# Reading the weights a second time for their range check, in six later turns

## The chip, the cores and the metric

The kernel runs on one core of a Trainium2 chip. The metric is the time on the device in microseconds (us). Names of engines: PE is TensorE, the matmul engine (PEld its weight loads), DVE is VectorE, ACT is ScalarE, POOL is GpSimd, SP is SyncE, which here only issues transfers. "SPq" and "ACTq" are the parts of SP and ACT that issue DMAs.

## The reference

Two layers follow each other. The first is a gated linear recurrence with 4 batch entries, 8 heads, 768 steps and head size 48; the second a gated state-space layer on 384 features with 512 inner channels:

```python
for t in range(S):
    state = alpha[:, :, t, :, None] * state + np.einsum('bhd,bhe->bhde', k[:, :, t], v[:, :, t])
    y[:, :, t] = np.einsum('bhd,bhde->bhe', q[:, :, t], state)
...
proj = x @ w_in
val, gate = (proj[..., :D_inner], proj[..., D_inner:])
for t in range(S):
    h = a[0, 0] * h + val[:, t, :]
    ys[:, t, :] = h
silu = gate * (1.0 / (1.0 + np.exp(-gate)))
return (silu * ys @ w_out).astype(np.float32)
```

`x` is `y` with the heads side by side. The weights `w_in`, `w_out` and `A_log` are handed over in their inputs' own types; the kernel reads `w_in` and `w_out` as pairs of 32-bit words and makes 32-bit floats of them itself.

## The kernel before

**Groups and turns.** The 4 x 768 steps are cut into N = 12 groups of 256 steps (NG = 3 groups for each batch entry). Work runs in turns: in turn n, the recurrence of group n is finished and that of group n + 1 begun, the first part of the second layer of group n - 1 runs, and the output of group n - 2. Group and turn numbers, and those of batch entries, count from 0.

**An order written by hand.** Each turn is a string of letters, read one by one (lines 467 to 517), and each engine runs its instructions in the order in which they are written there. F is a step of `front(n)`: scans along time of alpha (`V`, `P`), then q and k multiplied by them, scores `sc`, and k turned back (`tpk`, `Kn`). A is the same for group n + 1. B is a step of `back(n)`: block states `z`, values `y`, features `x_sb`, and their transposes `tpx`, `xT`. P and H are steps of `ssm(n - 1)`: twelve products `pj` with `w_in`, then the scan `hh` (DVE), the gate `sg` (ACT) and their product `f` (DVE). O is a step of `ssm(n - 2)`: products `o` with `w_out`, and the output. `pj` and `o` share two PSUM buffers.

**How inputs arrive.** Groups 0 to 3 (`n < BY_VECTOR`, line 229) are loaded by `load(n)` into `pads` and turned by TensorE (`tp`). Later groups come by whole batch entries, `load_batch(b)` at line 234, in a layout that VectorE turns by itself (`squares`, line 330). Entry 1 needs only its last two groups and is cut into 48 transfers; entries 2 and 3 have 12 each. All of these are issued by SP, in program order; v is loaded by ACT from turn 2 on. The letter L calls `load_later(n)`: the load of group n + 2 in turns 0 and 1, the last four weight units (turn 0), and entries 2 and 3 in turns 3 and 5. M calls `load_last(n)`: entry 1 in turn 2, and v of group n + 2. `load_batch` also has GpSimd fill unused columns (line 241).

**Shared buffers.** Two big buffers are used in turn. One holds `pads`, then entry 2. The other holds `staging`, the raw words of the twelve weight units (line 261), then entry 1, then entry 3. A new holder's transfers wait until the old one was last read.

**Weights.** U is `convert_unit`: two passes on ACT, two on DVE and one on GpSimd turn the raw words of a unit into 32-bit floats. W is `check_units(p)`: two ACT passes over the high words of WP = 3 units in `staging`, which sum up whether a weight is out of range. C is `check_products(n)`: two ACT passes over `V`, which do the same for the products of decays. At the end `any_outside` (line 447) looks at all these sums; if one is out of range, a slower general form computes everything again. It does not run for these inputs.

Of the kernel before, what the change touches and what calls it, by code (L numbers as in the profile page):

```python
# [9 lines left out]
FP32 = mybir.dt.float32  # L10
U8 = mybir.dt.uint8
U32 = mybir.dt.uint32
# [6 lines left out]
def kernel(  # L19
# [24 lines left out]
    nc = tc.nc  # L44
# [3 lines left out]
    C = 128  # L48
# [5 lines left out]
    NG = S // GC  # L54
# [3 lines left out]
    NK = DM // C  # L58
# [14 lines left out]
    w_out = const.tile([C, NI, DM], FP32, name="w_out")  # L73

    left = const.tile([C, N, 2], FP32, name="left")
    WP = 3
    left_w = const.tile([C, 3 * NI // WP, 2], FP32, name="left_w")
    flag = const.tile([1, 1], I32, name="flag")
    bias = const.tile([C, 3], FP32, name="bias")
# [3 lines left out]
    units = []  # L83
# [7 lines left out]
    def load_heads(dst, src, n, queue=nc.sync):  # L91

        b, g = divmod(n, NG)
        for c in range(G):
            rows = ds(g * GC + c * C, C)
            queue.dma_start(out=dst[:, c], in_=src[b, :, rows, :].rearrange("h p d -> p h d"))

    def load_pairs(dst, src, n, queue=nc.sync):

        b, g = divmod(n, NG)  # L100
        for c in range(G):
            rows = ds(g * GC + c * C, C)
            for i in range(2):
                queue.dma_start(out=dst[:, c, :, i, 0:D],
                                in_=src[b, ds(NP * i, NP), rows, :].rearrange("h p d -> p h d"))
# [93 lines left out]
    def step(gen):  # L199
        if gen is not None:  # L200
            next(gen, None)


    def ranged(ctx):
        def pool(name, bufs, **kw):
            return ctx.enter_context(tc.tile_pool(name=name, bufs=bufs, **kw))

        own = pool("own", 1)
        p1 = pool("p1", 1)
# [20 lines left out]
        W = 32  # L230
# [3 lines left out]
        def load_batch(b):  # L234
            t = big.tile([C, 3, NP * NW * W], FP32, tag=f"big{1 - b % 2}", name="batch")
            for m, (name, src) in enumerate((("a", alpha), ("q", q), ("k", k))):
                tv = t[:, m].rearrange("p (x e) -> p x e", e=W)
                batches[b, name] = t[:, m].rearrange("p (j x) -> p j x", j=NP)
                w0 = max(0, BY_VECTOR - NG * b) * GC // W
                for i in range(2):  # L240
                    nc.gpsimd.memset(tv[ds(DP * i + W, W), :, D - W:W], 1.0 if name == "a" else 0.0)  # L241
                for j, nj in [(0, NP)] if w0 == 0 else [(j, 1) for j in range(NP)]:
                    for i in range(2):
                        for half in range(2):
                            ch = min(W, D - W * half)
                            nc.sync.dma_start(  # L246
                                out=tv[ds(DP * i + W * half, W), j * NW + w0:(j + nj) * NW, 0:ch],
                                in_=src[b, ds(NP * i + j, nj), w0 * W:S, ds(W * half, ch)]
                                .rearrange("j (w p) d -> p (j w) d", p=W))
# [3 lines left out]
        def load(n, names="aqkv", queue=nc.sync):  # L253
            for name in names:
                if name == "v":
                    vs[n] = p3.tile([C, G, H, D], FP32, name="v_sb")
                    load_heads(vs[n], v, n, queue)
                elif n < BY_VECTOR:
                    load_pairs(pads[n % NBUF][name], dict(a=alpha, q=q, k=k)[name], n, queue)

        staging = big.tile([C, len(units), NK * C * 2], U32, tag="big0", name="staging")
# [8 lines left out]
        def convert_unit(u):  # L270


            lo, hi = bits_of(u)[..., 0], bits_of(u)[..., 1]
            dst = units[u][0].bitcast(U32)

            nc.scalar.activation(lo.bitcast(FP32), lo, AF.Copy, scale=2.0 ** -29, bias=2.0 ** 23)
            nc.scalar.activation(lo, lo.bitcast(FP32), AF.Copy, bias=-2.0 ** 23)
            nc.vector.tensor_scalar(out=dst, in0=hi, scalar1=0x07FFFFFF, scalar2=3,
                                    op0=ALU.bitwise_and, op1=ALU.logical_shift_left)
            nc.vector.scalar_tensor_tensor(out=dst, in0=hi, scalar=0xC0000000, in1=dst,  # L280
                                           op0=ALU.bitwise_and, op1=ALU.bitwise_or)
            nc.gpsimd.tensor_add(units[u][0].bitcast(I32), units[u][0].bitcast(I32), lo.bitcast(I32))

        def check_units(p):


            h = staging[:, ds(WP * p, WP), :].rearrange("p u (x two) -> p (u x) two", two=2)[:, :, 1].bitcast(FP32)
            nc.scalar.activation(h, h, AF.Square, scale=2.0 ** -16, accum_out=left_w[:, p, 0:1])
            nc.scalar.activation(h, h, AF.Relu, scale=-2.0 ** 60, bias=bias[:, 0:1], accum_out=left_w[:, p, 1:2])

# [86 lines left out]
        def check_products(n):  # L377
            V = Vs[n % 2]
            junk = p1.tile([C, NP, GC], U8, name="junk")
            nc.scalar.activation(junk, V[:, :, 0:GC], AF.Relu, scale=-1.0 / LOW, bias=bias[:, 0:1],  # L380
                                 accum_out=left[:, n, 0:1])
            nc.scalar.activation(junk, V[:, :, 0:GC], AF.Relu, scale=1.0 / HIGH, bias=bias[:, 2:3],
                                 accum_out=left[:, n, 1:2])
# [58 lines left out]
        for u in range(4, 8):  # L442
            fetch_unit(u)
        nc.scalar.activation(a_dec, a_log, AF.Exp)
        to_convert, to_check = iter(range(len(units))), iter(range(len(units) // WP))

        def any_outside():

            worst = own.tile([C, 1], FP32, name="worst")
            bad = own.tile([C, 3 * NI // WP * 2 + 1], FP32, name="bad")  # L450
            nc.vector.tensor_reduce(out=bad[:, 0:1], in_=left.rearrange("p n w -> p (n w)"),
                                    axis=mybir.AxisListType.X, op=ALU.max)

            nc.vector.tensor_scalar(out=bad[:, 1:], in0=left_w.rearrange("p n w -> p (n w)"), scalar1=0.5,
                                    scalar2=0.5, op0=ALU.is_lt, op1=ALU.is_lt)
            nc.vector.tensor_reduce(out=worst, in_=bad, axis=mybir.AxisListType.X, op=ALU.max)
            wt = ps_tp.tile([1, C], FP32, tag="tp", name="wt")
            nc.tensor.transpose(wt, worst, ident)
            w1 = own.tile([1, 1], FP32, name="w1")
            nc.vector.tensor_reduce(out=w1, in_=wt, axis=mybir.AxisListType.X, op=ALU.max)  # L460
            nc.vector.tensor_scalar(out=flag, in0=w1, scalar1=0.0, scalar2=None, op0=ALU.is_gt)
# [2 lines left out]

        early = ["FFFFLUFUFABBABB", "UUFPUUFHPUHFFPUHBBCPHABUAUBL", "FPUFHPUHFFPHBBCAPHBWAWOBWAWOM"]
        usual = "FLPHPHFFOABBCPHABPHBAOM"
        ending = ["PHPHOPHPHO", "OO"]
        fronts = {n: front(n) for n in range(N)}  # L470
        backs = {n: back(n) for n in range(N)}
# [11 lines left out]
        def load_last(n):  # L483
            if n == 2:
                load_batch(1)
            if 2 <= n < N - 2:
                load(n + 2, "v", nc.scalar)

        with tc.manual_schedule():
            for n in range(N + 2):  # L490
                if n == N:
                    any_outside()
                for word in early[n] if n < len(early) else usual if n < N else ending[n - N]:
                    if word == "F":
                        step(fronts[n])
                    elif word == "A":
                        step(fronts.get(n + 1))
                    elif word == "B":
                        step(backs[n])
                    elif word in "PH":  # L500
                        if n - 1 not in ssms:
                            ssms[n - 1] = ssm(n - 1, xs.pop(n - 1), prev_h, p2, ps_mm)
                        step(ssms[n - 1])
                    elif word == "O":
                        step(ssms[n - 2])
                    elif word == "C":
                        if n == 1:
                            check_products(0)
                        check_products(n)
                    elif word == "U":  # L510
                        convert_unit(next(to_convert))
                    elif word == "W":
                        check_units(next(to_check))
                    elif word == "L":
                        load_later(n)
                    elif word == "M":
                        load_last(n)
            outside = nc.values_load(flag[0:1, 0:1], min_val=0, max_val=1)
# [156 lines left out]
    with ExitStack() as inner:  # L675
        outside = ranged(inner)
# [33 lines left out]
```

## Time and profile before

| what | value |
|---|---|
| time, median of 3 runs | 335.95 us (334.61 to 337.5) |
| span of the profiled run | 334.8 us |
| PE busy | 291.8 us (87%) |
| DVE busy | 223.5 us (67%) |
| ACT busy | 126.0 us (38%) |
| POOL busy | 45.0 us (13%) |
| mean granted TensorE clock | 0.942 |
| DMA moved | 29.01 MB in 157570 packets, 150864 of them under 512 B |

The profile is a record of one execution. Its page cuts the span into 40 slices of 8.4 us, and each digit is the busy share of an engine in tenths; PEclk is the clock that TensorE was granted, in tenths. "The chain that ended last" goes back from the last instruction: from each to what released it. Lines of a timeline give start, duration, engine, source line, output <- inputs and the number of instructions, and in brackets the idle time before them and what ended it. A line of waits gives who waited for whom: us in total, how often, the longest.

Here the costliest group is that of the products `pj` (135.6 us busy), then `o` (67.9 us). The twelve conversions and the four checks of weights all lie in the first three turns.

### The profile page before, as it was taken

How to read it: one execution, taken by the hardware profiler on the slowest of the kernel's cores; microseconds unless marked ns; L12 is line 12 of the kernel's file. 1: busy time of each engine (PE TensorE's matmuls, PEld its weight loads, DVE VectorE, ACT ScalarE, POOL GpSimd, SP SyncE). 2: the span in 40 equal slices, each digit the busy share in tenths (PEclk: the TensorE clock that was granted, in tenths of full speed). 3: DMA queues.
4: the chain of work that ended last, by engine and by line, in shares of the span. 5: the costliest groups of instructions: out<-in, count | busy, mean ns of one | idle time of the engine just before them, and what ended most of it. 6: DMA issues, size and time to landing. Idle time of an engine off the chain costs nothing.

```text
span 334.8 us, 9254 instructions
## 1 busy us (share of the span) xinstructions
PE 291.8 (87%) x4041; PEld 231.6 (69%) x4041; DVE 223.5 (67%) x387; ACT 126.0 (38%) x259; POOL 45.0 (13%) x58
## 2 busy tenths in 40 slices
PE   1577995899499792599999999999999999999993
PEld 1355883787377671477787778877887778777771
DVE  1886786769123960679878888898788988833220
ACT  1133668237932410243252442513524325244111
POOL 4020420320069300000910000000000000000000
PEclk9995898699789898599999999999999999999999
DMA  9999994000056547976885996940030120000011
GB/s 129 224 223 239 204 222 86 0 3 4 23 104 99 72 74 99 125 101 94 116 117 108 132 120 99 153 79 31 2 72 25 28 46 25 25 26 2 27 45 59
DMA packets 157570, 29.01 MB, mean 87 GB/s; under 512 B 150864, under 2 KB 157008, under 8 KB 157520
## 3 DMA queue, kind: packets, MB, share of 16 engines
q1 hardware_dynamic: 134784, 20.06, 41.2%
q10 hardware_dynamic: 22736, 8.26, 10.1%
q8 instruction: 34, 0.56, 0.7%
q14 instruction: 16, 0.13, 0.1%
HBM read 23.60 MB, written 4.72 MB: 85 GB/s over the span
## 4 chain that ended last, share of the span: by engine, by line
PE 75%; DVE 6%; DMA 6%; ACT 5%; SPq 3%; issue 3%; ACTq 1%; DVEq 0%
PE pj L115 34%; PE o L130 18%; PE sc L368 4%; PE tp L326 4%; PE tpk L142 4%; PE y L187 4%; PE z L154 3%; PE y L169 3%; DMA v_sb<-in_v_dram 3%; PE tpx L196 3%; SPq L246 2%; DVE P L344 2%; DVE V L339 2%; DMA pads<-in_alpha_dram 1%; DMA batch<-in_q_dram 1%
## 5 line engine op out<-in xcount | busy, mean ns | idle before, releaser
L115 PE MATMUL pj<-xT,w_in 128*128 128x256 f32 x576 | 135.6, 389 | 0.0
L115 PEld LDWEIGHTS pj<-xT,w_in 128*128 128x128 f32 x576 | 109.7, 194 | 17.6 <-issue 0.2
L130 PE MATMUL o<-w_out,f 128*128 128x384 f32 x192 | 67.9, 499 | 0.0
L124 ACT ACTIVATE sg<-pj 128x256 f32<-128x256 f32 x48 | 18.4, 384 | 119.1 <-DVE hh L119 98.6
L130 PEld LDWEIGHTS o<-w_out,f 128*128 128x128 f32 x192 | 36.2, 197 | 20.9 <-issue 2.1
L119 DVE TENSOR_TENSOR_SCAN hh<-a_dec,hh,pj 128x256 f32<-128x256 f32 x32 | 23.7, 740 | 21.1 <-PE pj L115 21.1
L125 DVE TENSOR_TENSOR f<-sg,hh 128x256 f32<-128x256 f32 x48 | 20.4, 425 | 24.9 <-ACT sg L124 24.9
L326 PE MATMUL tp<-ident,pads 128*128 128x128 f32 x96 | 19.6, 358 | 16.0 <-DMA pads<-in_alpha_dram 6.9
L241 POOL MEMSET batch<- 32x1536 f32 x18 | 24.7, 1371 | 64.7 <-DMA out_dram<-o_sb 41.7
L326 PEld LDWEIGHTS tp<-ident,pads 128*128 128x128 f32 x96 | 15.0, 183 | 19.4 <-issue 8.0
L368 PE MATMUL sc<-Q,K 64*64 64x64 f32 x768 | 15.9, 237 | 10.7 <-DVE K L359 10.6
L133 ACT ACTIVATE o_sb<-o 128x384 f32<-128x384 f32 x24 | 11.8, 490 | 33.5 <-PE o L130 33.5
L368 PEld LDWEIGHTS sc<-Q,K 64*64 64x64 f32 x768 | 14.0, 148 | 14.9 <-issue 14.3
L344 DVE TENSOR_TENSOR_SCAN P<-aT,iV,bias 128x256 f32<-128x256 f32 x32 | 23.6, 780 | 0.6
L339 DVE TENSOR_TENSOR_SCAN V<-aT,bias 128x256 f32<-128x256 f32 x32 | 20.3, 677 | 0.3
L393 POOL TENSOR_TENSOR S_n<-S_end,V 128x192 f32<-128x192 f32 x7 | 4.2, 598 | 118.5 <-DVE V L339 118.5
L330 DVE STREAM_TRANSPOSE K<-batch 128x1024 f32<-128x1024 f32 x8 | 9.9, 1239 | 12.7 <-DMA batch<-in_k_dram 12.7
L196 PE MATMUL tpx<-ident,x_sb 128*128 128x128 f32 x72 | 11.9, 300 | 6.0 <-DVE P L344 4.3
L187 PEld LDWEIGHTS y<-S_n,Q 64*64 64x64 f32 x704 | 13.1, 140 | 5.7 <-issue 4.9
L169 PE MATMUL y<-v_sb,A 64*64 64x48 f32 x768 | 14.2, 220 | 3.2 <-issue 3.2
L371 DVE COPY_PREDICATED A<-mask,sc 128x512 f32<-128x512 uint8 x24 | 16.1, 723 | 0.7 <-PE sc L368 0.7
L154 PEld LDWEIGHTS z<-v_sb,Kn 64*64 64x64 f32 x768 | 12.3, 134 | 6.1 <-issue 5.4
(64 smaller groups left out, 314.2 us busy)
## 6 DMA issues: line engine op xcount, KB each, us to landing
out_dram<-o_sb ACTq DMA_DIRECT2D x24, 192.0 KB, 2.0
staging<-in_moe_w_in_dram SPq DMA_DIRECT2D x8, 384.0 KB, 5.0
v_sb<-in_v_dram ACTq DMA_DIRECT2D x16, 192.0 KB, 3.4
pads<-in_alpha_dram SPq DMA_DIRECT2D x16, 96.0 KB, 5.0
pads<-in_k_dram SPq DMA_DIRECT2D x16, 96.0 KB, 3.7
v_sb<-in_v_dram SPq DMA_DIRECT2D x8, 192.0 KB, 4.4
staging<-in_moe_w_out_dram SPq DMA_DIRECT2D x4, 384.0 KB, 5.5
batch<-in_alpha_dram SPq DMA_DIRECT2D x4, 384.0 KB, 6.6
```

The lines of the kernel that those rows point to most:

```text
L115: nc.tensor.matmul(pj[:, i, :], w_in[:, kk, i, ds(cc * C, C)], xT[:, kk, :], start=(kk == 0), stop=(kk == NK - 1))
L119: nc.vector.tensor_tensor_scan(out=hh, data0=a_dec[:, cc:cc + 1].to_broadcast([C, GC]), data1=pj[:, 0, :], initial=prev_h[cc][:, GC - 1:GC ...
L130: nc.tensor.matmul(o, f[:, cc, ds(c * C, C)], w_out[:, cc, :], start=(cc == 0), stop=(cc == NI - 1))
L154: nc.tensor.matmul(zv[chs, r, g, j, :], Kn[rows, g, j, chs], v_sb[rows, g, NP * i + j, :], start=True, stop=True, skip_group_check=True)
L169: nc.tensor.matmul(yv[at, i, c, j, :], A[rows, i, c * NP + j, :], v_sb[rows, c, NP * i + j, :], start=(c == 0 and j == 0), stop=False, ski ...
L187: nc.tensor.matmul(yv[at, i, c, j, :], Q[rows, j, ds(R * x, R)], S_n[rows, x, j, :], start=False, stop=(c == G - 1 and j == NP - 1), skip_ ...
L196: nc.tensor.transpose(tp[:, kk, :], x_sb[:, c, ds(kk * C, C)], ident)
L241: nc.gpsimd.memset(tv[ds(DP * i + W, W), :, D - W:W], 1.0 if name == "a" else 0.0)
L326: nc.tensor.transpose(tp[:, u, ds(c * C, C)], pad[name][:, c, j], ident)
L339: nc.vector.tensor_tensor_scan(out=V[:, 2 * jj + u, GC - 1::-1], data0=tp[:, u, ::-1], data1=bias[:, 1:2].to_broadcast([C, GC]), initial=1 ...
L344: nc.vector.tensor_tensor_scan(out=P[:, 2 * jj + u, :], data0=tp[:, u, :], data1=bias[:, 1:2].to_broadcast([C, GC]), initial=iV0[:, 2 * jj ...
L368: nc.tensor.matmul(scv[ds(R * r, R), i, c * NP + j, :], K[rows, j, steps], Q[rows, j, steps], start=True, stop=True, skip_group_check=True)
```

## The change

The check of the weights no longer reads `staging`. Instead the raw weights are fetched from memory a second time, two units at a time (WP = 2), into a buffer of their own (`part`, one buffer), and checked there, in six parts. Part p is fetched by the letter M of turn p + 4 and checked by the letter W, now the first of a turn, in turn p + 5; so the fetches fall into turns 4 to 9 and the checks into turns 5 to 10. `staging` is then free as soon as the last unit was converted, and M, with entry 1's load, moves up in turn 2, to just behind that conversion. The load of group 3 (L in turn 1) moves up as well. The check of group 0's products moves from turn 1 to turn 0.

```diff
-    WP = 3
+    WP = 2
...
-        def check_units(p):
-            h = staging[:, ds(WP * p, WP), :].rearrange("p u (x two) -> p (u x) two", two=2)[:, :, 1].bitcast(FP32)
+        parts = {}
+
+        def fetch_part(p):
+            parts[p] = p1.tile([C, WP, NK * C * 2], U32, name="part")
+            for w in range(WP):
+                dst, src = units[WP * p + w]
+                nc.sync.dma_start(out=parts[p][:, w].rearrange("p (a n) -> p a n", a=dst.shape[1]), in_=src.bitcast(U32))
+
+        def check_part(p):
+            h = parts.pop(p).rearrange("p u (x two) -> p (u x) two", two=2)[:, :, 1].bitcast(FP32)
             nc.scalar.activation(h, h, AF.Square, scale=2.0 ** -16, accum_out=left_w[:, p, 0:1])
             nc.scalar.activation(h, h, AF.Relu, scale=-2.0 ** 60, bias=bias[:, 0:1], accum_out=left_w[:, p, 1:2])
...
-        early = ["FFFFLUFUFABBABB", "UUFPUUFHPUHFFPUHBBCPHABUAUBL", "FPUFHPUHFFPHBBCAPHBWAWOBWAWOM"]
-        usual = "FLPHPHFFOABBCPHABPHBAOM"
+        early = ["FFFFLUFUFCABBABB", "UUFPUUFLHPUHFFPUHBBCPHABUAUB", "FPUFHPUHMFFPHBBCAPHBAOBAO"]
+        usual = "WFLPHPHFFOABBCPHABPHBAOM"
...
+            if 0 <= n - NG - 1 < len(units) // WP:
+                fetch_part(n - NG - 1)
...
                     elif word == "C":
-                        if n == 1:
-                            check_products(0)
                         check_products(n)
...
-                    elif word == "W":
-                        check_units(next(to_check))
+                    elif word == "W" and n - NG - 2 in parts:
+                        check_part(n - NG - 2)
```

More of the change, by code (lines that the diff above doesn't have):

```diff
@@ L444, in ranged @@
         nc.scalar.activation(a_dec, a_log, AF.Exp)
-        to_convert, to_check = iter(range(len(units))), iter(range(len(units) // WP))
+        to_convert = iter(range(len(units)))
         def any_outside():
```

## The prediction

> **What bounds the kernel now.** I read the page's 40 slices first, then the chain that ended last, in order of time, then the waits (all engines, and the DMA queue's own), then each engine's timeline from 40 to 182 us. The slices:
>
> ```profile
> PE   1577995899499792599999999999999999999993
> PEclk9995898699789898599999999999999999999999
> DMA  9999994000056547976885996940030120000011
> ```
>
> From slice 17 (142 us) to the end TensorE is full at full clock, so nothing off TensorE costs time there as long as nothing stops it. Before that it has holes, and DMA is silent in slices 7 to 10 (58 to 92 us). The chain shows a turn's rhythm and what makes the holes:
>
> ```profile
> 82.00 1.36 ACT staging L288 x2
> 83.38 1.43 ACT staging L289 x2
> 88.80 1.97 PE tp L326 x8
> 90.77 4.50 PE o L130 x8
> ...
> 105.49 2.93 DMA batch<-in_q_dram
> ...
> 132.64 2.64 DMA batch<-in_k_dram
> ...
> 156.56 5.18 PE pj L115 x24
> ...
> 178.34 5.18 PE pj L115 x24
> ```
>
> The pairs of products that open a turn (`pj` x24) stand at 156.56, 178.34, 200.11: a full turn costs 21.78 us. Turn 4 opens at 121.90, so turn 4 took 34.66; turn 2 (60.64 to 95.08, by its first transposes) 34.4 and turn 3 26.8. The waits tell why:
>
> ```profile
> SPq L246 <- ACT staging L289: 42.3, 1, 42.3
> SPq L246 <- DMA out_dram<-o_sb: 29.1, 7, 7.6
> SPq L246 <- DMA v_sb<-in_v_dram: 19.8, 7, 7.9
> ```
>
> These are the DMA queue's own waits (us in total, times, longest). TensorE's timeline has its idle time in brackets:
>
> ```profile
> 88.80 1.97 PE L326 MATMUL tp<-ident,pads 128*128 128x128 f32 x8 [4.28 <-ACT xT L197]
> ...
> 113.00 1.35 PE L187 MATMUL y<-S_n,Q 64*64 64x48 f32 x48 [1.74 <-DVE S_n L400]
> ...
> 137.81 2.07 PE L368 MATMUL sc<-Q,K 64*64 64x64 f32 x64 [10.57 <-DVE K L359]
> ```
>
> Batch entry 1 (the second, counted from 0) shares its buffer with `staging`, so SyncE waits 42.3 us until the last range check has read it (94.5 us). Then VectorE waits for alpha (4.19 us before 108.42) and for k (12.65 us before 135.69), and TensorE behind it.
>
> **What the Trainium skill says.** "PSUM — Partial Sum Buffer", section "Engine vs sequencer instructions": the queues of ScalarE, VectorE and GpSimd are strictly first in, first out. The trace agrees: `xT` (tile ready long before) runs on ACT at 88.25, after checks from 82.00 to 87.33. "DMA: Bandwidth & Descriptors", section "Anatomy of one DMA": DMA engines wait on no semaphore, the issuing sequencer does, before dispatch. The trace agrees (SPq's 42.3 us), so all that stands behind a waiting issue on SyncE waits too. Same page, "Queues, rings and completion order": each DMA engine consumes a ring's descriptors in ring order, so a weight part issued after a batch lands after it; no run here shows that yet. "TensorE: Matmul & The Clock Gate", "What's actually happening": an idle TensorE is throttled to half clock. The trace agrees: after the wait at 137.81 the 64 score products took 2.07 us, against 1.16 at 161.67. Price: "ScalarE: Activation LUTs", "What ACT_TABLE_LOAD costs", gives 0.833 ns per element; here, two passes over 1152 columns took 2.72 us (82.00 to 84.72), so over 768 columns about 2.72 - 2 x 384 x 0.833 ns = 2.1 us, an estimate.
>
> **The change, part by part.**
>
> *Check of group 0's products, turn 1 to turn 0.* Turn 1 has four passes on ACT from 48.91 to 53.9; two leave. VectorE waited 2.03 us for `sg` behind them, of which 0.45 is usual: 1.6 us saved. In turn 0 the two (2.6 us) fall in ACT's idle 5.88 us ahead of the fence at 27.04: free.
>
> *Fourth group's load called sooner.* SyncE ran ahead and issued it at 40.28 to 52.2 already, and its first transposes are at 75.94: 0.
>
> *Twelve-unit checks out of turn 2.* TensorE's wait of 4.28 goes, and the slow clock behind it: `tp` x8 1.97 for 1.04, `o` x8 4.69 for 2.75. Sum 4.28 + 0.9 + 1.9 = 7.1 us. The other two checks (89.0 to 94.5) lay beside `o`.
>
> *Batch entry 1 sooner.* `staging` is now free after the last weight conversion, GpSimd's add at 70.5 to 71.5, less 1.6: SyncE starts at 70 and not 94.95. Its 48 issues took 38.2 us (94.95 to 133.1), of which 12.5 us were waits for landing outputs and v (waits in windows); 48 x 0.53 = 25.5 are left, and I take 3 us of such waits: done at 99. Needed: alpha in turn 3 (about 97), q at its end, k at turn 4's start (about 109). All are in time, alpha by 80. That saves turn 3's 1.74 plus its slow products (`pj` 4.54 for 2.75, `y` 0.3): 3.9 us; and turn 4's 10.57 plus 1.0 (`sc`), 0.9 (`tpk`), 0.3 (`o`): 12.8 us (check: 34.66 - 21.78 = 12.9).
>
> Sum of gains: 1.6 + 7.1 + 3.9 + 12.8 = 25.4 us. Turn 5 would open at 156.56 - 25.4 = 131.2.
>
> *Weights read again.* 12 x 384 KB = 4.7 MB more. Volume isn't the trouble: 786 KB a turn. The place is: the parts are issued by SyncE, in program order behind entry 2 (called in turn 3) and, for part 1, behind entry 3 (called at the start of turn 5). Their checks open turns 5 to 10 on ACT; a check whose part hasn't landed holds up `sg`, so VectorE's `f`, so the PSUM buffers of `pj`, so TensorE.
>
> How long is an entry? Four alpha issues of entries 2 and 3 took 8.17 and 7.71 us, so twelve about 24; entry 3 took 34.8 (7.71 + 16.55 + 10.54) with 9.9 of waits: 25 again. DMA is saturated then (share 1.03 in 178.34 to 200.11). A last issue lands about 7 us later (6.5 to 8.6 us in the windows).
> - Entry 2: its buffer (`pads`) is free at turn 3's start (about 87), so it follows entry 1: 99 + 25 + 4 of waits for outputs = 128. Part 0 is issued by 129, lands 7 us of queue and 1 us of data later, 137, check until 139. Today `sg` comes 4.4 us after a turn opens (160.98 against 156.56), that is 135.6. TensorE has two `pj`, `sc` and `tpk` to do, 5.18 + 1.09 + 1.02 = 7.3 us, to 138.5. Cost about 1 us.
> - Entry 3 waits for group 5's K transpose, 2.4 us into turn 5 (157.72 + 1.24): start 134, 25 + 4 of waits, 163. Part 1 issued at 164, landed 172, checked until 174, `sg` 174.5. Turn 6 opens at 132.2 + 21.8 = 154.0 and TensorE has work to 161.3: idle 13.2 us, then slow clock as in turn 4, 2.2. Cost 15.4 us.
> - Parts 2 to 5: each is issued when the buffer is free, a turn ahead, with no entry in front. Today ACT is idle from 158.72 to 160.98 ahead of `sg`, 2.26 us against a check of 2.1: 0.
>
> Sum: 25.4 - 1 - 15.4 = 9.0 us gained, 335.95 - 9.0 = 327. The bounds of the unknown: part 1 at 166 (no waits in either entry) gives 321, at 180 gives 335.
>
> **Rivals.**
> *The parts come in time (no stall over 5 us).* For: their bytes are few, and the parts have a turn's time by the source. Against: SyncE's order, and entry 3 alone needs 25 us where turn 5 has 21.8. 335.95 - 25.4 = 310.5, up to 316.
> *The gain is eaten.* The queue slips by some 8 to 12 us over three entries, each issue waiting for an output that waits for a turn: 333 to 339. For: the 29.1 and 19.8 us of such waits above. Against: entries are now issued earlier than the outputs that they waited for.
> *Slower.* The entries take what they take now: 38.2, 40.0 and 34.8. Entry 1 ends at 108, part 0 lands at 156, entry 3 starts at 149 and ends at 184, part 1 lands at 193, checked 195: turn 6 works as if opened at 195.5 - 7.3 + 2.2 = 190.4, against 178.34: 348. For: nothing in the diff removes those waits. Against: with ACT stopped at a check, no later output can stand ahead of the part that it waits for, so the waits are cut short.
>
> **How the numbers follow.** Late part 1, 321 to 332.5: 0.55, time 327. Parts in time, 310 to 320: 0.20. Gain eaten, 333 to 339: 0.13. Slower: 0.12. The range 314 to 338 leaves out a third of the second case and the last one. Faster by over 1% (under 332.6): 0.75; within: 0.13; slower: 0.12.
>
> **What would show it.** Gone: SPq's 42.3 us on `staging`, VectorE's waits for alpha and k, the hole in slice 15. Turn 4 without a wait of TensorE. New: ACT waiting for a DMA of `part` ahead of the first pass in turn 6, over 10 us, about 1 us or little more in turn 5 and none later, and a dip of PEclk behind it. Wrong if the wait for parts is spread over more than two turns, if entry 1 still comes late for k, or if VectorE's `f` after the checks of turns 7 to 10 makes TensorE wait.

## The result and the profile after

| | before | after |
|---|---|---|
| time, median | 336.03 us | 359.51 us |
| ratio, 95% interval | | 1.0608 (1.0502 to 1.0713) |
| span of the profiled run | 334.8 us | 356.1 us |
| PE busy | 291.8 us | 292.3 us |
| mean granted TensorE clock | 0.942 | 0.919 |
| DMA moved | 29.01 MB | 33.74 MB |

The change makes the kernel 6.1% slower. TensorE has as much work as before; it waits longer. (Ratios leave out the slower runs of a kernel, here two of the four after the change, so they need not be those of the medians.) The slices of the changed kernel, 8.9 us each:

```profile
PE   2558995986999699705991099999999999999994
PEclk9995996999999989955998579999999999999998
DMA  9999981095434999999999730503205030000002
```

Slices count from 0. The old hole (slices 15 and 16 of before) has shrunk to a dip at slice 13. DMA, which rested from about 58 to 94 us before, starts again at 70. But there are two new holes, in slices 17 and 21 to 22. TensorE's timeline of the changed kernel, with the idle time before each line in brackets, names them:

```profile
123.56 1.68 PE L377 MATMUL sc<-Q,K 64*64 64x64 f32 x64 [3.29 <-DVE K L368]
...
164.39 5.10 PE L130 MATMUL o<-w_out,f 128*128 128x384 f32 x8 [14.98 <-ACT sg L124]
...
204.02 5.49 PE L130 MATMUL o<-w_out,f 128*128 128x384 f32 x8 [15.33 <-ACT sg L124]
```

The wait for k at 137.81 (10.57 us) is down to 3.29. Twice, in turns 5 and 6, TensorE waits some 15 us for the gate `sg`, and the eight products behind each wait take 5.10 and 5.49 us instead of 2.75. The chain that ended last shows what `sg` was behind:

```profile
156.44 5.46 DMA part<-in_moe_w_in_dram
161.99 1.00 ACT part L297 x2
163.01 1.06 ACT part L298 x2
164.39 5.10 PE o L130 x8
...
196.74 4.88 DMA part<-in_moe_w_in_dram
201.64 0.98 ACT part L297 x2
202.64 1.06 ACT part L298 x2
204.02 5.49 PE o L130 x8
...
221.59 5.18 PE pj L115 x24
```

The two checks that open turns 5 and 6 run at 162.0 and 201.6, as soon as their parts have landed. ACT has stood in front of them for 19.34 and 19.72 us, by its timeline:

```profile
161.99 0.90 ACT L297 ACTIVATE part<-part 128x768 f32<-128x768 f32 x1 [19.34 <-DMA part<-in_moe_w_in_dram]
...
201.64 0.88 ACT L297 ACTIVATE part<-part 128x768 f32<-128x768 f32 x1 [19.72 <-DMA part<-in_moe_w_in_dram]
```

Turn 7 opens at 221.59, against 200.11 before; from there on both kernels take 21.8 us a turn.

Turn by turn: turn 5 opens at 142.1 (the `o` products at its edge end at 139.53 + 2.60) and not at 156.56, a gain of 14.4 us. Turn 5 then takes 39.3 and turn 6 40.2 us instead of 21.8 each, a loss of 35.9. The net loss, 21.5 us, is the difference of the spans (21.3). Why the parts land so late stands in the issues of SyncE (start, us, instruction, how many):

```profile
70.63 10.87 SPq L246 DMA_DIRECT2D batch<-in_alpha_dram  x16
81.55 16.37 SPq L246 DMA_DIRECT2D batch<-in_q_dram  x16
97.96 21.53 SPq L246 DMA_DIRECT2D batch<-in_k_dram  x16
119.59 9.22 SPq L246 DMA_DIRECT2D batch<-in_alpha_dram  x4
128.85 11.88 SPq L246 DMA_DIRECT2D batch<-in_q_dram  x4
140.78 13.19 SPq L246 DMA_DIRECT2D batch<-in_k_dram  x4
154.02 3.44 SPq L291 DMA_DIRECT2D part<-in_moe_w_in_dram  x2
157.56 10.52 SPq L246 DMA_DIRECT2D batch<-in_alpha_dram  x4
168.12 12.33 SPq L246 DMA_DIRECT2D batch<-in_q_dram  x4
186.30 8.13 SPq L246 DMA_DIRECT2D batch<-in_k_dram  x4
194.52 32.41 SPq L291 DMA_DIRECT2D part<-in_moe_w_in_dram  x6
```

Entry 1 takes 48.9 us, entry 2 34.4, entry 3 37. Part 0 can only be issued at 154.0 and part 1 at 194.5. SyncE's own waits, over the whole run:

```profile
SPq L246 <- DMA out_dram<-o_sb: 35.1, 8, 6.5
SPq L246 <- POOL w_out L282: 18.3, 1, 18.3
```

The 42.3 us on `staging` have become 18.3, up to the last unit's conversion. The waits for landed outputs have grown from 29.1 to 35.1 us, and those for v have fallen from 19.8 to 4.6. What counts is where they lie. In entry 1, from 82 to 98 us and from 98 to 120 us, they are:

```profile
SPq L246 <- DMA out_dram<-o_sb: 8.3, 2, 4.4
SPq L246 <- DMA out_dram<-o_sb: 12.1, 2, 6.5
```

With 2.2 us for v that makes 22.6 us of waits in entry 1, where there were 12.5 before. Entry 1 takes 48.9 us to issue for 38.2, so these waits are nearly all of the difference. (They come with the program. In the trace the transfers of SP and ACT name eight completion semaphores in rotation, so that a transfer waits for the eighth before it, whoever issued that one.)

### The profile page after: what moved, and what is told of

Read it like the earlier page. It is cut to its first block, busy times and chain, and to the rows that moved or that the text cites. A ratio compares the mean times of both kernels' runs of the same rounds, so it can differ in the third digit from the quotient of the medians.

```text
span 356.1 us, 9281 instructions
## 1 busy us (share of the span) xinstructions
PE 292.3 (82%) x4041; PEld 229.9 (65%) x4041; DVE 223.1 (63%) x387; ACT 127.8 (36%) x267; POOL 44.5 (12%) x58
## 2 busy tenths in 40 slices
DMA packets 161347, 33.74 MB, mean 95 GB/s; under 512 B 151056, under 2 KB 160272, under 8 KB 161296
## 4 chain that ended last, share of the span: by engine, by line
PE 66%; DVE 9%; DMA 9%; SPq 5%; ACT 4%; POOL 3%; issue 2%; ACTq 0%; DVEq 0%; POOLq 0%
PE pj L115 27%; PE o L130 18%; DMA v_sb<-in_v_dram 4%; PE z L154 3%; SPq L246 3%; PE y L187 3%; PE tp L335 3%; PE y L169 3%; DMA part<-in_moe_w_in_dram 3%; PE tpk L142 3%; PE sc L377 3%; DVE P L353 2%; POOL batch L241 2%; PE tpx L196 2%; DVE V L348 2%
## 5 line engine op out<-in xcount | busy, mean ns | idle before, releaser
L115 PE MATMUL pj<-xT,w_in 128*128 128x256 f32 x576 | 133.3, 384 | 0.0
L115 PEld LDWEIGHTS pj<-xT,w_in 128*128 128x128 f32 x576 | 108.1, 192 | 16.9 <-issue 0.2
L130 PE MATMUL o<-w_out,f 128*128 128x384 f32 x192 | 71.2, 519 | 30.3 <-ACT sg L124 30.3
L130 PEld LDWEIGHTS o<-w_out,f 128*128 128x128 f32 x192 | 37.4, 204 | 52.8 <-ACT sg L124 30.8
L124 ACT ACTIVATE sg<-pj 128x256 f32<-128x256 f32 x48 | 18.4, 383 | 90.2 <-DVE hh L119 86.3
L335 PE MATMUL tp<-ident,pads 128*128 128x128 f32 x96 | 18.8, 346 | 12.6 <-DMA pads<-in_alpha_dram 7.0
L297 ACT ACTIVATE part<-part 128x768 f32<-128x768 f32 x6 | 5.5, 917 | 46.0 <-DMA part<-in_moe_w_in_dram 39.1
L377 PEld LDWEIGHTS sc<-Q,K 64*64 64x64 f32 x768 | 13.2, 141 | 7.8 <-issue 6.6
L154 PEld LDWEIGHTS z<-v_sb,Kn 64*64 64x64 f32 x768 | 12.5, 136 | 7.1 <-issue 6.1
L411 DVE TENSOR_TENSOR S_n<-S_n,z 128x192 f32<-128x192 f32 x32 | 11.2, 350 | 8.4 <-POOL S_n L402 4.6
```

The lines of the kernel that those rows point to most:

```text
L115: nc.tensor.matmul(pj[:, i, :], w_in[:, kk, i, ds(cc * C, C)], xT[:, kk, :], start=(kk == 0), stop=(kk == NK - 1))
L130: nc.tensor.matmul(o, f[:, cc, ds(c * C, C)], w_out[:, cc, :], start=(cc == 0), stop=(cc == NI - 1))
L154: nc.tensor.matmul(zv[chs, r, g, j, :], Kn[rows, g, j, chs], v_sb[rows, g, NP * i + j, :], start=True, stop=True, skip_group_check=True)
L335: nc.tensor.transpose(tp[:, u, ds(c * C, C)], pad[name][:, c, j], ident)
L377: nc.tensor.matmul(scv[ds(R * r, R), i, c * NP + j, :], K[rows, j, steps], Q[rows, j, steps], start=True, stop=True, skip_group_check=True)
```

## The experiments

**Theory.** ACT, SyncE and the entries form a chain: a check at the head of ACT's turn waits for a part, the part stands on SyncE behind an entry, and the entry waits for outputs. **Rivals.** The second reading of the weights loads the DMA engines too much, wherever it stands; the passes of the checks cost too much on ACT; or the loss lies in the early turns.

**no_parts.** The change without fetches and checks of parts (the sums of the checks are filled with zeros once instead).

```diff
-            if 0 <= n - NG - 1 < len(units) // WP:
-                fetch_part(n - NG - 1)
```

> Leaves out the range check of the weights: no part is fetched and none is checked; all else is as in the changed kernel. Changed kernel 359.5 us; its turns 5 and 6 took 39.2 and 40.2 us instead of 21.8, together 35.8 us over. Queue theory (a check on ACT waits for a part that stands on SyncE behind a whole batch entry): these 35.8 go, 324 us. Traffic theory (4.7 MB more on busy DMA engines slow everything): the same 324 or less. A third theory, that the loss lies in the earlier turns (entry 1 still late for k, GpSimd's fills ahead of its state product): over 335 us, since that loss stays.

325.5 us, ratio to before 0.9728 (0.9687 to 0.9769). So the parts cost 34.0 us by the medians and 35.7 by the profiled spans, as the two long turns said, and the early load with all the rest of the change is worth 2.7%. The theory of the early turns falls. The queue and the traffic theory forecast the same here, so this run can't tell them apart.

**part1_ahead.** A second buffer, and part 1 called together with part 0, ahead of entry 3.

```diff
-            parts[p] = p1.tile([C, WP, NK * C * 2], U32, name="part")
+            parts[p] = p2.tile([C, WP, NK * C * 2], U32, name="part")
...
-                fetch_part(n - NG - 1)
+            if n == NG + 1:
+                fetch_part(0)
+            if 0 <= n - NG < len(units) // WP and n > NG:
+                fetch_part(n - NG)
```

> Two buffers for parts, and part 1 is called with part 0 in turn 4, so that it stands on SyncE ahead of entry 3; part 0 still stands behind entry 2. Queue theory: turn 5 still waits (17 us over), turn 6 does not: 359.5 - 18.4 = 341 us, and the wait of ACT for a part is one of about 19 us, not two. Traffic theory: both waits stay in some form, 355 to 360 us.

348.84 us, 1.0400 (1.0358 to 1.0442), between the two forecasts. ACT's timeline, its first pass over each of the first three parts:

```profile
164.56 0.90 ACT L297 ACTIVATE part<-part 128x768 f32<-128x768 f32 x1 [19.14 <-DMA part<-in_moe_w_in_dram]
...
186.00 0.94 ACT L297 ACTIVATE part<-part 128x768 f32<-128x768 f32 x1 [1.71 <-issue]
...
214.41 0.88 ACT L297 ACTIVATE part<-part 128x768 f32<-128x768 f32 x1 [8.35 <-DMA part<-in_moe_w_in_dram]
```

Part 1, now ahead of entry 3, is there in time, and part 0, still behind entry 2, is not. What I had missed is part 2: it is now the one behind entry 3 and comes 8.35 us late. The order on SyncE decides which check waits.

**parts_late.** All weights, in four parts of three units, fetched in turns 6 to 9 and checked first in turns 7 to 10.

```diff
-    WP = 2
+    WP = 3
...
-                fetch_part(n - NG - 1)
+                fetch_part(n - NG - 3)
...
-                        check_part(n - NG - 2)
+                        check_part(n - NG - 4)
```

> The same weights are fetched and checked, in four parts of three units, fetched in turns 6 to 9 (called behind entry 3) and checked at the start of turns 7 to 10. Queue theory: no batch entry stands ahead of a part for longer than a turn, about 324 us, at most 4 us for a last piece of entry 3 before part 0. Traffic theory: the same bytes beside the same turns' outputs, so most of the 35.8 us stays, over 345 us. ACT theory (the passes themselves, some 10 us in all, hold up the gates): over 332 us.

344.98 us, 1.0312 (1.0251 to 1.0373): at the edge of what the traffic theory had forecast, 21 us above the queue theory. The time alone would speak for traffic; ACT's timeline, its first passes over parts 0 and 1, does not:

```profile
205.00 1.21 ACT L297 ACTIVATE part<-part 128x1152 f32<-128x1152 f32 x1 [18.40 <-DMA part<-in_moe_w_in_dram]
...
227.58 1.29 ACT L297 ACTIVATE part<-part 128x1152 f32<-128x1152 f32 x1 [1.76 <-issue]
```

ACT waits 18.40 us, once, for part 0, and TensorE 14.68 us behind it. Entry 3 is issued from 167.0 to 197.4, ten us into turn 7, so part 0 is still behind it. My step of "at most 4 us" was wrong, the mechanism wasn't. Parts 1 to 3, with as many bytes each, are not waited for, which speaks against the traffic theory.

**check_late_in_turn.** Fetches as in the change; the check moves to a later place in the turn.

```diff
-        usual = "WFLPHPHFFOABBCPHABPHBAOM"
+        usual = "FLPHPHFFOABBCPHABWPHBAOM"
```

> The change with one letter moved: W stands late in the turn (behind the features' copies on ACT) and no longer first. Fetches, sizes and queues are as in the change. Queue theory (ACT stands at a check while TensorE's gates queue behind it): part 0 lands at about 161 us, when turn 5 (open from 142) has reached the new place at about 158, so its wait falls from 19.3 to 3 us or so; part 1 (landing about 195 to 202, turn 6 open from 167) still waits, 10 to 15 us, and TensorE's waits of 15.0 and 15.3 us fall to 0 to 3 and 8 to 13: 338 to 350 us. If the loss comes from busy DMA engines and not from where ACT stands: 355 to 360 us.

349.88 us, 1.0419 (1.0359 to 1.0479). TensorE's timeline:

```profile
168.63 5.45 PE L115 MATMUL pj<-xT,w_in 128*128 128x256 f32 x24 [2.37 <-ACT xT L197]
209.71 8.05 PE L115 MATMUL pj<-xT,w_in 128*128 128x256 f32 x24 [18.90 <-ACT xT L197]
```

The first wait falls from 14.98 to 2.37 us, as forecast. The second was to fall to 8 to 13 us and grows from 15.33 to 18.90: part 1 lands when SyncE has issued entry 3, and a turn 6 that comes to its check sooner just waits there longer. Removing one wait feeds the next, as long as the landing of part 1 sets the end.

**parts_act.** The six parts issued by ACT, each behind the check of the one before.

```diff
-                nc.sync.dma_start(out=parts[p][:, w]...
+                nc.scalar.dma_start(out=parts[p][:, w]...
...
+                        if 0 <= n - NG - 1 < len(units) // WP:
+                            fetch_part(n - NG - 1)
```

> Six parts as in the change, in the same turns, but issued by ACT on its own queue right behind the check of the part before (part 0 at the start of turn 4), and so no longer behind the entries on SyncE. Queue theory: each part lands within its turn, 324 to 330 us (12 issues of 0.6 us on ACT, and the two queues share the engines). Traffic theory: parts and entries still share the same DMA engines in turns 4 to 6, over 345 us.

353.19 us, 1.0547 (1.0513 to 1.0581): far above the queue theory, within the traffic theory. No check waits any more (idle ahead of them 1.7 us each), yet most of the loss is there. VectorE's timeline shows the new waits, for k of entries 1 and 2:

```profile
128.81 1.25 DVE L339 STREAM_TRANSPOSE K<-batch 128x1024 f32<-128x1024 f32 x1 [9.69 <-DMA batch<-in_k_dram]
...
187.85 1.25 DVE L339 STREAM_TRANSPOSE K<-batch 128x1024 f32<-128x1024 f32 x1 [12.85 <-DMA batch<-in_k_dram]
```

Entries 2 and 3 took 56 and 65 us to issue, and SyncE waited 74.6 us for outputs in the whole run. Freed from the parts, SyncE met more waits of the other kind. Whether those waits or the shared engines made the entries so slow, this run can't tell; it only shows that another queue for the parts is no cure.

**before_no_check.** The kernel before without its four checks of weights, nothing moved (their sums are filled with zeros once).

```diff
-                        check_units(next(to_check))
+                        pass
```

> The kernel before with the four checks of weights left out and nothing else changed: entry 1's load stays where it was called, at the end of turn 2, behind GpSimd's state product of that turn. SyncE has nothing else to issue, so entry 1 starts when the last unit is converted, at about 71 us, as in the change. If freeing the buffer is the whole gain: about 322 us (no_parts 325.5, less about 5 us since no fills stand ahead of the state product, plus 1.6 us for the products' check in turn 1). If the earlier call is what brings the gain: about 335 us, as before.

318.41 us, 0.9498 (0.9450 to 0.9546): less than no_parts (325.5). SyncE's first issues of entry 1:

```profile
71.66 9.32 SPq L247 DMA_DIRECT2D batch<-in_alpha_dram  x16
```

Entry 1 starts there although its call stands at the end of turn 2. The early call gains nothing: SyncE runs ahead by itself as soon as the buffer is free.

**no_parts_vec.** no_parts, with the state product of turn 2 on VectorE.

```diff
-                vg = nc.vector if n < 2 else nc.gpsimd
+                vg = nc.vector if n < 3 else nc.gpsimd
```

> no_parts (325.5 us), with the state product of group 2 on VectorE instead of GpSimd, so that it no longer stands behind six fills of entry 1 on GpSimd. Fill theory: VectorE's wait of 4.64 us in turn 2 goes, and as the last transfers of k follow an output of turn 3, they come sooner by as much: 319 to 322 us. Load theory (SyncE's own pace brings k at 120.8 us whatever turn 2 does): 325 us.

320.77 us, 0.9563 (0.9498 to 0.9628), 4.7 us below no_parts. In the changed kernel, and in no_parts alike, the early call had put GpSimd's six fills ahead of that product. GpSimd's and then VectorE's timeline of the changed kernel:

```profile
70.66 8.42 POOL L241 MEMSET batch<- 32x1536 f32 x6
79.16 0.51 POOL L402 TENSOR_TENSOR S_n<-S_end,V 128x192 f32<-128x192 f32 x1
```

```profile
79.71 1.13 DVE L411 TENSOR_TENSOR S_n<-S_n,z 128x192 f32<-128x192 f32 x3 [4.64 <-POOL S_n L402]
```

The 4.64 us are gone in no_parts_vec. The interval overlaps that of before_no_check, so nothing else of the moves can be told from noise.

**after_out_pool and after_outv_pool.** The changed kernel with its outputs, and then with v's loads too, issued by GpSimd, whose transfers name eight other completion semaphores in the trace.

```diff
-            nc.scalar.dma_start(out=out[b, ds(g * GC + c * C, C), :], in_=o_sb)
+            nc.gpsimd.dma_start(out=out[b, ds(g * GC + c * C, C), :], in_=o_sb)
...
-                load(n + 2, "v", nc.scalar)
+                load(n + 2, "v", nc.gpsimd)
```

> The changed kernel with its outputs issued by GpSimd instead of ACT, whose transfers count on completion semaphores of their own; SyncE's transfers then share theirs with v's loads only. Output theory (SyncE's issues of the entries wait for outputs that end turns): entry 1 in 35 us or less instead of 48.9, part 0 lands some 10 us sooner, part 1 too; 340 to 350 us. Bytes theory (the DMA engines set the entries' pace): entries and time as before, 355 to 362 us. GpSimd's fills and state products may wait behind outputs, which would cost either theory a few us.

363.96 us, 1.0868 (1.0801 to 1.0935). Both theories miss: SyncE's waits for outputs are gone from the entries, but one wait of 21.1 us for v, loaded at the end of turn 3, has taken their place, and entry 1 takes 49 us again.

> As after_out_pool, with v's loads of turns 2 to 9 on GpSimd too: SyncE's transfers share completion semaphores with nobody. It makes true the assumption of the prediction that the entries take 25 to 29 us each. Output theory: entry 1 about 26 us, entry 2 about 25, part 0 lands near 140 us and part 1 near 175; two waits for parts of 3 to 8 and 10 to 16 us; 327 to 336 us, the upper end for the fills ahead of the state product. Bytes theory: 355 to 362 us.

347.90 us, 1.0360 (1.0294 to 1.0425). SyncE's issues:

```profile
70.74 9.50 SPq L246 DMA_DIRECT2D batch<-in_alpha_dram  x16
80.28 10.13 SPq L246 DMA_DIRECT2D batch<-in_q_dram  x16
90.46 9.53 SPq L246 DMA_DIRECT2D batch<-in_k_dram  x16
100.09 9.21 SPq L246 DMA_DIRECT2D batch<-in_alpha_dram  x4
109.34 11.63 SPq L246 DMA_DIRECT2D batch<-in_q_dram  x4
121.02 14.14 SPq L246 DMA_DIRECT2D batch<-in_k_dram  x4
135.21 2.84 SPq L291 DMA_DIRECT2D part<-in_moe_w_in_dram  x2
143.18 11.63 SPq L246 DMA_DIRECT2D batch<-in_alpha_dram  x4
```

Entry 1 now takes 29.3 us: the 20 us over that were waits for ACT's transfers at the end of turns. TensorE no longer waits for k in turn 4. Entry 2, though, takes 35.1 us with no such wait at all, and entry 3 38.2. For entry 2 that is 36864 packets at 0.95 ns, at a DMA share of 1.23; that the DMA engines are the limit then is a reading of this share, not shown by a run of its own. Part 0's check waits 1.21 us, part 1's 24.37 (at 188.9), TensorE 19.98. With both of these entries 6 to 13 us longer than the forecast's 25 to 29, the time is 12 us over its upper end.

Three of these kernels wait for part 1 at the start of turn 6. From the landing of part 1 to the end of the span they need 154.5 us (changed kernel, 201.6 to 356.1), 157.7 (after_out_pool) and 157.3 (after_outv_pool). The landing of part 1 sets the time.

**no_parts_whole.** no_parts_vec with entry 1 loaded whole, in 12 transfers instead of 48.

```diff
-                w0 = max(0, BY_VECTOR - NG * b) * GC // W
+                w0 = 0
```

> no_parts_vec with entry 1 loaded whole, all three groups, in 12 transfers rather than 48: half as many bytes again (36864 packets for 24576), a quarter of the issues. Output theory (SyncE's waits for landed outputs, not bytes, made entry 1 take 48.9 us): k lands before turn 4, VectorE's wait for k (4.7 us) and the slow clock behind it go, 5 us below no_parts_vec. Bytes theory: entry 1 takes longer still, and the time is above no_parts_vec.

317.28 us, 0.9499 (0.9430 to 0.9567). Entry 1 takes 37.5 us (70.68 to 108.14) with half as many packets again, and TensorE's wait of 3.4 us for k is gone. 3.5 us below no_parts_vec, as the output theory had it, though the intervals overlap.

**parts_later_vec and best.** All weights checked. The first fetches four parts in turns 7 to 10 and checks them first in turns 8 to 11. The second fetches in turns 6 to 9 and checks late in turns 7 to 10, with entry 1 whole. Both have three units a part and the state product on VectorE. Of the second's edits, those on place:

```diff
-        usual = "WFLPHPHFFOABBCPHABPHBAOM"
+        usual = "FLPHPHFFOABBCPHABWPHBAOM"
...
-                fetch_part(n - NG - 1)
+                fetch_part(n - NG - 3)
...
-                        check_part(n - NG - 2)
+                        check_part(n - NG - 4)
```

> All weights checked, in four parts of three units, fetched in turns 7 to 10 and checked at the start of turns 8 to 11, and the state product of group 2 on VectorE. In parts_late only part 0 came late (18.4 us), since entry 3 was still being issued until 197 us, ten us into turn 7. Queue theory: no entry is left ahead of part 0, so no wait; checks of 2.7 us against 2.3 us of idle ACT cost nothing or 0.4 us each: as no_parts_vec plus 0 to 2 us. Traffic theory: over 335 us.

324.57 us, 0.9601 (0.9537 to 0.9664), some 2 us above the queue theory. In the profiled run part 0 comes 8.37 us late once more, this time not behind entry 3 (issued by 200) but since its own issue waits until 207.3 for transfers at the end of turn 7. That run took 326.52 us, near the top of the five (321.37 to 326.6); whether the faster ones waited as long isn't known.

> All checks kept: four parts of three units, fetched at the end of turns 6 to 9, checked late in turns 7 to 10 (behind the features' copies, where ACT is idle for 2.5 us), state product of group 2 on VectorE, entry 1 loaded whole in 12 transfers. Queue theory: no part is waited for, as no_parts_whole (317.3 us) plus 0 to 2 us: 317 to 320. If the checks themselves cost (4 x 2.7 us): up to 328.

317.85 us, 0.9477 (0.9420 to 0.9533), 5.2% faster than before and 11.6% below the median of the changed kernel, with every check in place. Its one hole behind turn 2:

```profile
198.06 7.13 PE L115 MATMUL pj<-xT,w_in 128*128 128x256 f32 x24 [4.06 <-ACT xT L197]
```

Part 0 still comes 4.7 us late; the other checks are not waited for. It differs from no_parts_whole (317.28) only in the parts, and the intervals overlap. So the second reading and its checks, well placed, cost nothing that can be measured, against the traffic and the ACT theory.

## Why the prediction was wrong

It forecast 327 us; 359.5 was measured, above the whole range. The mechanism was the one forecast for part 1: ACT waits for a part behind an entry, with a slow clock behind the wait and nothing in later turns. For part 0 the prediction had about 1 us of it. That this mechanism makes the loss is shown by no_parts, part1_ahead, check_late_in_turn and best. The sizes failed. Between the profiled spans, gains of 14.4 us came where 25.4 were forecast, and stalls of 35.9 where 16.4 were. By these steps:

- **"48 x 0.53 = 25.5 are left, and I take 3 us of such waits: done at 99."** This is the step that failed first, and the later ones follow from it. Entry 1 had 22.6 us of waits in place of 3 and took 48.9 us, to 119.5. The argument that "entries are now issued earlier than the outputs that they waited for" was false: an entry that starts a turn sooner waits for the outputs of the sooner turn. ACT issued the outputs of turns 2 and 3 at 86.63, 93.01, 103.77 and 115.65 us, and each of entry 1's four waits for outputs ended 2 us behind one of these. after_outv_pool shows it too: without ACT's transfers in the rotation entry 1 takes 29.3 us, next to the 28.5 forecast.
- **"Twelve about 24 ... 25 again" for an entry.** I scaled the four alpha issues, which are the quickest: in entry 2 of after_outv_pool, where nothing was waited for, alpha, q and k took 9.2, 11.6 and 14.1 us. Right behind entry 1, an entry took 35.1 us there. (After a rest of SyncE it can be less: entry 3 of parts_late took 30.4, with 3 us of waits.) I also took entry 3's 34.8 us less its waits as pure work, but while SyncE waits the engines work on, so waits and work can't be subtracted. And of the 9.9 us of waits 7.6 lay ahead of the entry's first issue at 181.05; its own came to 9.2, so the sum was near by luck. The engines' share was 1.21 in that stretch of the changed kernel (119.6 to 154.0 us).
- **Part 0 "issued by 129 ... cost about 1 us".** It was issued at 154.0: 20 us from entry 1 and 5 from entry 2. Landing 8 us behind the issue was right (161.9). The cost was 39.3 - 21.8 = 17.5 us, the largest single miss.
- **Part 1 "issued at 164, landed 172 ... 15.4 us".** Issued at 194.5, landed 201.6; cost 18.4 us. The stall was sized nearly right, but by luck: its turn opened 27 us later than forecast (181.4 for 154.0) and the part landed 30 us later, so that the difference stayed.
- **Turn 1, "1.6 us".** VectorE's wait of 2.03 us for `sg` fell to the usual 0.45, as said, but turn 2 opened only 0.6 us sooner (60.04 for 60.64).
- **Turn 2, "7.1 us".** It went from 34.4 to 32.4. The hole at 88.80 is gone, but the fills ahead of the state product cost 4.64 us on VectorE. I had not asked what stands on GpSimd behind the moved call. before_no_check, without the move, has turn 3's first products of weights at 89.6 us, the changed kernel at 93.3.
- **Turn 4, "12.8 us".** It went from 34.66 to 27.0, that is 7.7: k of entry 1 came late again, with 3.29 us of waiting and the slow clock behind it. Its last transfers had waited for the last output of turn 3 (issued at 115.65). The prediction had named a late k as a sign of being wrong.
- **Turn 3, "3.9 us".** 26.8 to 22.7: right. The load of group 3 brought nothing, as said, and a check took 2.08 us for the estimate of 2.1, by the Trainium skill's "ScalarE: Activation LUTs", "What ACT_TABLE_LOAD costs"; it was hidden in turns 7 to 10, as said.

The rival "Slower" came nearest: with the entries as long as before (38.2, 40.0, 34.8) it had part 1 land at 193, for 348 us. I gave it 0.12 on an argument that no line of the profile carried. One thing is open: in parts_act, whether waits or shared engines made the entries slower still.

## What to carry to other kernels

A transfer is as late as all that stands ahead of it on the queue that issues it, and the engine that waits for it holds up all that stands behind on its own. So new loads go behind the long ones, and their consumers late, where the waiting engine is idle anyway. Before a call is moved ahead, list what it puts in front of others on every engine it uses, also the small fills. A wait seen before the change is not gone because the stage comes sooner: if it is for an event of the same turn, it moves along.

## What the runs showed of the hardware

The rate for small rows was lower than I had reckoned: in after_outv_pool 36864 packets of 64 and 128 B were issued in 35.1 us without a wait of SyncE, 0.95 ns each, at about 100 GB/s, beside v and outputs on GpSimd's queue. In the changed kernel the issue of a transfer of entry 2 or 3 took SyncE up to 4.3 us, but the first of an entry 0.4 us; one unit of weights took 2.38 us to issue behind entry 2, and another 0.37 with no entry ahead. So a long issue need not be work on SyncE: a transfer of the same size is issued fast when nothing is outstanding, which looks like the engines' pace.

The Trainium skill's "TensorE: Matmul & The Clock Gate", "What's actually happening", has an idle TensorE at half clock; the runs agree. In the changed kernel the clock was 0.50 in the 8 us without a product, and eight products `o` behind the wait took 5.10 us against 2.75. The changed kernel by stretches of time, and last the stretch of entry 2 in after_outv_pool, with the busy time of PE, PEld, DVE, ACT and POOL, then clock, DMA share and GB/s (a share over 1 is more packet time than 16 engines have, so that packets overlap):

```profile
119.60:154.00 34.40, 26.48 (x410) 20.91 (x408) 21.52 (x35) 8.38 (x18) 8.74 (x7) 0.92 1.21 119
154.00:162.00 8.00, 0.00 (x0) 0.00 (x0) 0.00 (x0) 0.01 (x1) 0.00 (x0) 0.50 1.43 170
...
100.00:135.30 35.30, 35.21 (x615) 27.99 (x614) 28.22 (x50) 14.01 (x30) 9.88 (x11) 1.00 1.23 128
```
